# Loading w_mod in three pieces and c in two loads, at the head of a decode block

## The chip, the cores and the metric

The kernel runs on one core of a Trainium2 chip. The core has five engines that work side by side: TensorE (PE; its weight loads are listed as PEld), VectorE (DVE), ScalarE (ACT), GpSimd (POOL) and SyncE (SP). 16 DMA engines move data between the chip's main memory (HBM) and the core's on-chip memory (SBUF, 128 partitions). The metric is the device time of one execution in microseconds, as the median of several runs.

## The reference

One block of a transformer in decode: 2 batch rows of 512 numbers each, adaptive layer norm from a condition `c`, attention over the last 4096 positions of a cache, and a feed-forward network.

```python
mod = (silu(c) @ w_mod).reshape(2, 6, 1, 512)        # w_mod: 512 x 3072
sa, ca, ga, sb, cb, gb = (mod[:, i] for i in range(6))
h = layernorm(x) * (1 + ca) + sa
q = h @ wq                                           # 512 x 4096: 32 heads of 128
o = softmax(q k^T / sqrt(128)) v                     # 8 K/V heads, last 4096 of 32768 positions
x = x + ga * (o @ wo)                                # 4096 x 512
h = layernorm(x) * (1 + cb) + sb
out = x + gb * (silu(h @ w1) @ w2)                   # 512 x 1792, 1792 x 512
```

All numbers are 32-bit floats. The weights and the part of the cache that is read come to about 97.5 MB, and each byte is used for two batch rows only.

## The kernel before

All large operands pass through one ring in SBUF: the tile `slots`, eight slots of 4096 floats in each of the 128 partitions. `stream(n)` hands out the next n slots (a pair or a group of four starts at a multiple of its size). `load_runs` (the load is line 93) loads `per` consecutive rows of a weight matrix into each partition; `load_pair` (line 82) loads two heads of the K or V cache. All these loads are issued on SP's queue, in the order in which the program names them, and a load whose slots are still in use waits on SP until the last reader is done. So SP's order is: w_mod (three slots), x, wq (slots 4 to 7), then K and V pairs by turns, wo in two parts, w1 in two, w2 in four, and the output.

For `w_mod`, partition p takes rows 4p to 4p+3, that is 4 x 3072 floats or 49,152 bytes which lie together in HBM. The view `wm[:, k, :]` is the k-th of these four rows.

`c` and `x` are small and are laid out with 128 columns in a few partitions of the tile `xc`, which a memset on DVE (line 100) clears first. Row b of `c` goes to partitions 16b, 16b+32, 16b+64 and 16b+96. Before the change, each batch row is loaded by two DMAs of two partitions (lines 105 and 106), issued on ACT's queue; x follows on SP's queue (line 109), behind w_mod.

The head of the computation is a chain. DVE transposes c into `cT` (line 261, in the helper `turned`), `silu_exp` (lines 228 to 231) and line 267 make `scT = silu(c)` transposed. Then PE multiplies it with w_mod: for each k, four products into `m_a` (line 275: the two modulations that the first norm needs, columns 0 to 1023 of the row) and four into `m_sp` (line 278: the other four, columns 1024 to 3071). After k = 0 the moments of x are put in between. DVE makes `h_a` (lines 286 to 290) and its transpose `hq_T`, and PE multiplies it with wq (line 308). Then the attention runs over eight steps, each with one K pair and one V pair: DVE transposes K (line 367), PE makes the scores (line 380), and after the softmax PE weights V (line 454). At the end come the products with wo (line 584), w1 (line 623) and w2 (line 657 for its first eight parts, lines 667 and 682 for the rest), the last element-wise work on DVE (lines 690 to 698) and the store (line 700).

The order on each engine around the change is the program's, as the scheduler of the tile framework lays it out. It waits for each reader's data by region of a tile. The first slots of the ring are reused by the first K pair, so SP's third large load waits for the products at lines 275 and 278.

Of the kernel before, what the change touches and what calls it, by code (L numbers as in the profile page):

```python
# [13 lines left out]
P = 128  # L14
B, D = 2, 512
# [8 lines left out]
def adaln_block(  # L24
# [19 lines left out]
    nc = tc.nc  # L44
# [16 lines left out]
    def const(shape, name):  # L61
        return consts.tile(shape, F32, name=name)

    def bank(tag, name):
        return (psum1 if tag in "CO" else psum).tile([P, 512], F32, tag=tag, name=name)
# [4 lines left out]
    def stream(n=1):  # L70
        i = turn_of[0]
        if n % 2 == 0:
            i += -i % n
        turn_of[0] = i + n
        return slots[:, i % RING : i % RING + n, :].rearrange("p s e -> p (s e)")
# [12 lines left out]
    def load_runs(w, per, lo, hi):  # L88

        e = w.shape[1]  # L90
        n = -(-(hi - lo) * e // 4096)
        t = stream(n)[:, : (hi - lo) * e].rearrange("p (q e) -> p q e", e=e)
        nc.sync.dma_start(t, w.rearrange("(p q) e -> p q e", q=per)[:, lo:hi, :])
        return t


    x2 = x.rearrange("b s d -> (b s) d")
    xc = const([P, 2, P], "xc")
    x_sp, c_sp = xc[:, 0, :], xc[:, 1, :]
    nc.vector.memset(xc, 0.0)  # L100
    wm = load_runs(w_mod, 4, 0, 4)
    rows8 = lambda t: t.rearrange("(ab r) m -> ab r m", r=16)[:, 0, :]
    for b in range(B):
        for lo in (0, 2):
            nc.scalar.dma_start(
                c_sp.rearrange("(g y) m -> g y m", g=4)[lo : lo + 2, 16 * b, :],
                c[b].rearrange("(g m) -> g m", m=P)[lo : lo + 2],
            )
    nc.sync.dma_start(rows8(x_sp), x2.rearrange("b (g m) -> g b m", m=P))  # L109
    wqt = load_runs(wq, 4, 0, 4)  # L110

# [470 lines left out]
    for q in range(32):  # L582
        g = q % 4
# [71 lines left out]
    for tt in range(WIDE):  # L655
        g = tt % 4
# [7 lines left out]
    y = bank("D", "acc_y")[:, :P]  # L664
# [13 lines left out]
    for tt in range(11, T2):  # L678
        for h in range(2):
            for g in range(4):  # L680
                lo = g * P + h * H
# [46 lines left out]
```

## Time and profile before

| what | value |
|---|---|
| time, median of 3 runs | 235.58 us (235.47 to 235.92) |
| the profiled execution, first to last instruction (span) | 233.6 us |
| median less span | 2.0 us |
| PE busy | 163.9 us (70%) |
| DVE busy | 115.2 us (49%) |
| ACT busy | 33.5 us (14%) |
| SP's DMA queue, share of 16 engines' time | 97.2% |
| HBM read | 97.53 MB, 418 GB/s over the span |
| mean granted clock of TensorE | 0.925 |

The profile gives the profiled execution's time as its span; what lies around the span isn't in it. The span is cut into 40 slices of 5.84 us in the page's second part. A busy PE is not PE at its peak, since matmuls are pipelined. The time of a DMA runs from its issue, on the queue of the engine that issued it, to its landing, when the last of its bytes is in place; a load that is issued while earlier ones are still under way waits its turn behind them.

### The profile page before, as it was taken

Reading aid. Unit: us, or ns where it says so; the run is one execution under the profiler, and the core shown is the slowest. Engines: PE = TensorE matmul, PEld = TensorE weight load, DVE = VectorE, ACT = ScalarE, POOL = GpSimd, SP = SyncE. Lnnn points to the kernel's source line nnn. Section 1 sums busy time; section 2 is a strip of 40 time slices with the busy share of each in tenths; the row PEclk is TensorE's granted clock in tenths of the full one; section 3 lists DMA queues with packets and bytes.
Section 4 is the critical chain, followed back from the end, with each engine's and each line's share of the span. In section 5 each row is a group of like instructions: output and inputs, shape, how many; then the busy total and the mean of one; then the engine's idle time right before and its main releaser. Section 6 shows DMA issues by size and latency. Waiting matters only on the chain.

```text
span 233.6 us, 2452 instructions
## 1 busy us (share of the span) xinstructions
PE 163.9 (70%) x998; PEld 41.1 (18%) x998; DVE 115.2 (49%) x180; ACT 33.5 (14%) x90; POOL 10.1 (4%) x34
## 2 busy tenths in 40 slices
PE   0004906959697839797598769748759786799984
PEld 0001401301111111211110201201111122233322
DVE  0007230187894758695197189259559540200332
ACT  2000210000311120130310201111030041000321
POOL 3004610000000000000000000000000000000000
PEclk9999995999859985999979979999997999899999
DMA  7998998999999999999999999999999999989991
GB/s 269 438 551 359 404 494 359 446 445 415 410 432 449 446 443 404 421 438 446 449 438 404 426 431 449 449 421 410 424 449 449 443 424 438 466 356 438 423 409 63
DMA packets 3794, 97.68 MB, mean 418 GB/s; under 512 B 432, under 2 KB 456, under 8 KB 968
## 3 DMA queue, kind: packets, MB, share of 16 engines
q1 hardware_dynamic: 3768, 97.53, 97.2%
q8 instruction: 8, 0.13, 0.2%
q14 instruction: 2, 0.02, 0.0%
q10 hardware_dynamic: 16, 0.00, 0.0%
HBM read 97.53 MB, written 0.00 MB: 418 GB/s over the span
## 4 chain that ended last, share of the span: by engine, by line
DMA 61%; issue 17%; DVE 13%; PE 6%; POOL 0%; SPq 0%; POOLq 0%; ACT 0%; DVEq 0%
DMA slots<-in_A_k_cache_dram 22%; DMA slots<-in_A_wq_dram 15%; DMA slots<-in_B_w_dram 12%; DMA slots<-in_A_v_cache_dram 12%; DVE kT L367 11%; PE q L308 3%; PE o L454 2%; DVE zp L426 1%; PE acc_yw L657 1%; DVE xp L424 1%; PE acc_l L682 0%; PE acc_y L667 0%; DVE qT L321 0%; POOL qg L325 0%; SPq L109 0%
## 5 line engine op out<-in xcount | busy, mean ns | idle before, releaser
L367 DVE STREAM_TRANSPOSE kT<-slots 128x1024 f32<-128x1024 f32 x64 | 73.7, 1211 | 22.7 <-DMA slots<-in_A_k_cache_dram 22.6
L380 PE MATMUL s<-kT,qbd 128*32 128x512 f32 x256 | 68.5, 714 | 17.6 <-DVE kT L367 16.6
L454 PE MATMUL o<-slots,ptb 128*32 128x512 f32 x256 | 29.1, 595 | 1.1 <-DMA slots<-in_A_v_cache_dram 1.1
L380 PEld LDWEIGHTS s<-kT,qbd 128*32 128x32 f32 x256 | 9.8, 115 | 69.1 <-DVE kT L367 65.1
L275 PE MATMUL m_a<-slots,scT 128*32 128x256 f32 x32 | 4.4, 500 | 20.6 <-DVE scT L267 20.6
L308 PE MATMUL q<-slots,hq_T 128*32 128x512 f32 x64 | 9.3, 745 | 7.7 <-DMA slots<-in_A_wq_dram 7.7
L554 PE MATMUL junk<-quad,id 128*32 128x512 f32 x24 | 12.9, 672 | 0.0
L466 ACT ACTIVATE ob<-o,own 128x128 f32<-128x128 f32 x32 | 9.1, 368 | 23.9 <-PE o L454 23.9
L410 ACT COPY bias<-bp 128x1 f32<-128x1 f32 x8 | 1.3, 159 | 75.3 <-PE bp L408 75.3
L454 PEld LDWEIGHTS o<-slots,ptb 128*32 128x32 f32 x256 | 7.7, 109 | 16.3 <-issue 16.2
L390 DVE TENSOR_REDUCE mx<-s 128x1 f32<-128x512 f32 x8 | 5.5, 692 | 9.6 <-PE s L380 9.6
L441 ACT ACTIVATE ptb<-pT,odd 128x256 f32<-128x256 f32 x16 | 6.7, 477 | 23.1 <-PE pT L433 23.1
L474 PE MATMUL o_all<-ob,selh 128*64 128x512 f32 x16 | 8.7, 622 | 2.0 <-ACT ob L466 2.0
L426 DVE TENSOR_TENSOR zp<-xp,quarter 128x1024 f32<-128x1024 f32 x8 | 9.8, 1226 | 0.2
L261 DVE STREAM_TRANSPOSE cT<-xc 128x128 f32<-128x128 f32 x1 | 0.4, 402 | 16.8 <-DMA xc<-in_c_dram 16.8
L321 DVE STREAM_TRANSPOSE qT<-q 128x512 f32<-128x512 f32 x2 | 1.4, 716 | 13.8 <-PE q L308 11.9
L433 PE MATMUL pT<-zp,mix 128*32 128x256 f32 x64 | 5.9, 446 | 2.8 <-DVE zp L426 2.3
L584 PE MATMUL acc_o<-slots,oTn 128*32 128x512 f32 x64 | 7.7, 593 | 0.0
L600 DVE STREAM_TRANSPOSE aoT<-ao 128x128 f32<-128x128 f32 x1 | 0.3, 316 | 14.8 <-PE ao L571 14.8
L392 PE MATMUL mT<-ident,mx 128*1 128x128 f32 x16 | 3.0, 271 | 6.4 <-DVE mx L390 6.4
L424 DVE STREAM_TRANSPOSE xp<-pr 128x512 f32<-128x512 f32 x8 | 5.5, 685 | 3.4 <-ACT pr L412 3.4
L278 PE MATMUL m_sp<-slots,scT 128*32 128x512 f32 x32 | 6.6, 712 | 0.0
(138 smaller groups left out, 90.1 us busy)
## 6 DMA issues: line engine op xcount, KB each, us to landing
slots<-in_A_k_cache_dram SPq DMA_DIRECT2D x8, 4096.0 KB, 27.6
slots<-in_A_v_cache_dram SPq DMA_DIRECT2D x8, 4096.0 KB, 27.8
slots<-in_w_mod_dram SPq DMA_DIRECT2D x1, 6144.0 KB, 17.0
slots<-in_A_wo_dram SPq DMA_DIRECT2D x1, 6144.0 KB
slots<-in_B_w_dram SPq DMA_DIRECT2D x1, 2688.0 KB
slots<-in_A_wo_dram SPq DMA_DIRECT2D x1, 2048.0 KB, 29.5
slots<-in_B_w_dram SPq DMA_DIRECT2D x1, 2048.0 KB
slots<-in_B_w_dram SPq DMA_DIRECT2D x1, 896.0 KB
```

The lines of the kernel that those rows point to most:

```text
L278: nc.tensor.matmul(m_sp[r, :], scT[:, k, :], cd[:, g], start=(k == 0), stop=(k == 3))
L308: nc.tensor.matmul(q_ps[n][32 * g : 32 * g + 32, :], hq_T[:, k, :], wv[:, n, g], start=(k == 0), stop=(k == 3),)
L367: inorder(nc.vector.transpose(kT[s, j][:, 32 * c : 32 * c + 32, :], kt[s].rearrange("p (n j r) -> p j n r", j=4, r=32)[:, j, 32 * c : 32 * ...
L380: inorder(nc.tensor.matmul(s_ps[s][r : r + 32, :], qbd[h // 4][:, h % 4, b, j, :], kT[s, j][:, 32 * c : 32 * c + 32, e:32:2], start=(j == ...
L424: inorder(nc.vector.transpose(xp, pr[s]))
L426: inorder(nc.vector.tensor_mul(zp, xp[:, None, :, 0:16].to_broadcast([P, 4, 16, 16]), quarter[:, :, None, None].to_broadcast([P, 4, 16, 16 ...
L441: inorder(nc.scalar.activation(ptb[s % 2][:, :, e, :], tp.rearrange("p (w z) -> p w z", z=16), AF.Copy, scale=odd[:, e : e + 1],))
L454: inorder(nc.tensor.matmul(o_ps[s][r : r + 32, :], ptb[s % 2][:, w].rearrange("p e z -> p (e z)"), vt[s].rearrange("p (c w m f d) -> p c f ...
L466: inorder(nc.scalar.activation(o_sb[s][:, c], o_ps[s][:, c], AF.Copy, scale=own[:, m : m + 1]))
L474: inorder(nc.tensor.matmul(o_all, selh[:, lo : lo + 2 * HQ], o_sb[s], start=(s == 0), stop=(s == STEPS - 1)))
L554: inorder(nc.tensor.matmul(junk[0:32, :], id4, quad.rearrange("p m y -> p (m y)"), start=True, stop=True,))
L584: inorder(nc.tensor.matmul(acc[32 * g : 32 * g + 32, :], oTn[:, q, :], wot[q], start=(q < 4), stop=(q >= 28),))
```

## The change

A new function `load_mod` takes the place of `load_runs` for w_mod. It takes the same three slots, and fills them by three loads instead of one. Two of them bring the first 6,144 bytes (1536 floats, half of the first of the four rows) of each partition's part, one for the 64 even partitions and one for the 64 odd ones. The third brings the other 43,008 bytes of all 128 partitions. All three are issued on SP's queue, ahead of x and wq as before. Each batch row of c is loaded by one DMA of four partitions instead of two DMAs of two, on ACT's queue as before. The computation is the same.

```diff
+    def load_mod():
+        FIRST = 3 * D
+        t = stream(3)[:, : 4 * 6 * D]
+        runs = w_mod.rearrange("(p q) e -> p (q e)", q=4)
+        for parity in range(2):
+            nc.sync.dma_start(
+                t.rearrange("(u y) e -> u y e", y=2)[:, parity, :FIRST],
+                runs.rearrange("(u y) e -> u y e", y=2)[:, parity, :FIRST],
+            )
+        nc.sync.dma_start(t[:, FIRST:], runs[:, FIRST:])
+        return t.rearrange("p (q e) -> p q e", q=4)
...
-    wm = load_runs(w_mod, 4, 0, 4)
+    wm = load_mod()
     rows8 = lambda t: t.rearrange("(ab r) m -> ab r m", r=16)[:, 0, :]
     for b in range(B):
-        for lo in (0, 2):
-            nc.scalar.dma_start(
-                c_sp.rearrange("(g y) m -> g y m", g=4)[lo : lo + 2, 16 * b, :],
-                c[b].rearrange("(g m) -> g m", m=P)[lo : lo + 2],
-            )
+        nc.scalar.dma_start(
+            c_sp.rearrange("(g y) m -> g y m", g=4)[:, 16 * b, :],
+            c[b].rearrange("(g m) -> g m", m=P),
+        )
     nc.sync.dma_start(rows8(x_sp), x2.rearrange("b (g m) -> g b m", m=P))
     wqt = load_runs(wq, 4, 0, 4)
```

## The prediction

> **What bounds the kernel now.** I read the page first: the stretches, the queues, the chain that ended last. The first row below is the DMA rate in 40 slices of 5.84 us, the next the loads' queue, then instruction fetches, and the last two the chain by engine and by line.
>
> ```profile
> DMA  7998998999999999999999999999999999989991
> GB/s 269 438 551 359 404 494 359 446 445 415 410 432 449 446 443 404 421 438 446 449 438 404 426 431 449 449 421 410 424 449 449 443 424 438 466 356 438 423 409 63
> ...
> q1 hardware_dynamic: 3768, 97.53, 97.2%
> q8 instruction: 8, 0.13, 0.2%
> ...
> DMA 61%; issue 17%; DVE 13%; PE 6%; POOL 0%; SPq 0%; POOLq 0%; ACT 0%; DVEq 0%
> ```
>
> The 16 DMA engines are busy 97.2% of the span with SP's loads. Only the first slice (269 GB/s) and the last (63) are low. So the kernel is one stream of 97.53 MB, and its end is the start of the stream, plus bytes over rate, plus a tail. To see both ends I asked for busy time in chosen windows (last columns: granted clock, DMA share, GB/s).
>
> ```profile
> 0.00:1.70 1.70, 0.00 (x0) 0.00 (x0) 0.27 (x1) 0.00 (x0) 1.09 (x8) 1.00 0.00 0
> 1.70:2.00 0.30, 0.00 (x0) 0.00 (x0) 0.00 (x0) 0.00 (x0) 0.30 (x2) 1.00 5.38 1638
> 2.00:3.00 1.00, 0.00 (x0) 0.00 (x0) 0.00 (x0) 0.00 (x0) 0.50 (x1) 1.00 0.81 295
> 3.00:4.00 1.00, 0.00 (x0) 0.00 (x0) 0.00 (x0) 0.18 (x1) 0.00 (x0) 1.00 0.00 0
> 4.00:5.00 1.00, 0.00 (x0) 0.00 (x0) 0.00 (x0) 1.00 (x1) 0.00 (x0) 1.00 1.83 786
> 36.20:200.00 163.80, 126.71 (x694) 27.27 (x694) 101.04 (x119) 25.41 (x77) 0.97 (x4) 0.91 1.01 433
> 216.00:226.00 10.00, 9.07 (x56) 2.79 (x54) 3.74 (x18) 3.61 (x6) 0.00 (x0) 1.00 0.98 415
> 228.00:229.60 1.60, 1.60 (x53) 1.21 (x53) 0.09 (x1) 0.65 (x2) 0.00 (x0) 1.00 0.43 169
> ```
>
> A share above 1 shows that the view books a transfer whole in the window where it starts. That makes the start readable. One row of w_mod is 49,152 bytes. 1638 GB/s in 0.30 us is 491 KB, so 10 rows start by 2.0 us; 295 KB is 6 more by 3.0 us; 786 KB is the second row of all 16 engines, after 4.0 us. Durations follow: 5.38 x 16 x 0.30 / 10 = 2.58 us for each of the first ten, 0.81 x 16 / 6 = 2.16 us for the six late ones, 1.83 x 16 / 16 = 1.83 us in steady state. The cold start costs (10 x 0.75 + 6 x 0.33) / 16 = 0.59 us on an engine's mean, beside 1.7 us in which nothing flows. From 36.2 to 200 us the rate is 433 GB/s, and the sixteen loads of K and V (listed below) lie in that window, so loads queued behind each other leave no gap. 97.53 MB at 433 GB/s is 225.2 us; from 1.7 us that ends at 226.9, and in the window from 228 us engines still finish (share 0.43). An engine carries what it lost at the start to the end, since nothing lets it catch up.
>
> The chain in order of time gives the tail, and its beginning gives the head:
>
> ```profile
> 1.94 35.14 DMA slots<-in_A_wq_dram
> 37.08 0.14 issue
> 37.22 5.87 PE q L308 x32
> ...
> 197.16 29.02 DMA slots<-in_B_w_dram
> 226.17 0.14 issue
> 226.31 1.92 PE acc_yw L657 x16
> ...
> 230.79 0.14 DVEq L724
> ```
>
> The last matmuls start when the first part of w2 lands at 226.17. Of the waits below, PE waited 0.7 us for that load: compute there is that much ahead, and a stream that shifts by less shifts the end one to one.
>
> ```profile
> PE acc_yw L657 <- DMA slots<-in_B_w_dram: 0.7, 1, 0.7
> ```
>
> **The change part by part.** The head of the kernel, from the timeline (start, length, engine, line):
>
> ```profile
> 0.73 0.37 SPq L93 DMA_DIRECT2D slots<-in_w_mod_dram  x1
> 1.16 2.63 ACTq L105 DMA_DIRECT2D xc<-in_c_dram  x4
> 1.17 0.72 SPq L109 DMA_DIRECT2D xc<-in_A_x_dram  x1
> 1.94 0.58 SPq L93 DMA_DIRECT2D slots<-in_A_wq_dram  x1
> 17.91 0.40 DVE L261 STREAM_TRANSPOSE cT<-xc 128x128 f32<-128x128 f32 x1 [16.78 <-DMA xc<-in_c_dram]
> 20.55 1.08 PE L275 MATMUL m_a<-slots,scT 128*32 128x256 f32 x8 [20.55 <-DVE scT L267]
> 28.30 1.83 SPq L82 DMA_DIRECT2D slots<-in_A_k_cache_dram  x2
> 29.91 0.40 DVE L261 STREAM_TRANSPOSE hq_T<-h_a 128x128 f32<-128x128 f32 x1
> ```
>
> The page's list of issues has the time from issue to landing in its last column:
>
> ```profile
> slots<-in_A_k_cache_dram SPq DMA_DIRECT2D x8, 4096.0 KB, 27.6
> slots<-in_A_v_cache_dram SPq DMA_DIRECT2D x8, 4096.0 KB, 27.8
> slots<-in_w_mod_dram SPq DMA_DIRECT2D x1, 6144.0 KB, 17.0
> ```
>
> *c earlier.* c is issued from 1.16 us and arrives at 17.9, with the whole of w_mod (0.73 + 17.0 = 17.7). Half as many loads, beside rows of 6,144 bytes instead of 49,152, should pass much sooner; I take 4 to 10 us. DVE then finishes scT (now 17.91 to 20.5, so 2.6 us of work) before w_mod has landed, and m_a starts at 17.7 instead of 20.55: 2.8 us sooner. The four first matmuls of k = 0 read only columns 0 to 1023 and could start on the first two loads, but the next ones read columns up to 3071 and wait for the third. What follows moves by those 2.8 us: the K loads' issue from 28.30 to 25.5, hq_T from 30.3 to 27.5. Neither is late now. The projection at line 308 waits for wq until 37.08, 6.8 us after hq_T; the K loads stand behind wq in the queue. Worth 0.0 us; cover gone would mean that hq_T came later than 37.08.
>
> The Trainium skill's page "DMA: Bandwidth & Descriptors" (section "Queues, rings and completion order") says that a DMA engine takes turns between queues packet by packet. That would explain c's arrival with w_mod and its gain here; the sum is zero with or without it.
>
> *Two more issues on SP.* They stand ahead of x's and wq's issue. At 0.37 to 0.72 us each these move by 0.7 to 1.4 us; wq goes out by 3.4 us and is first needed when w_mod's bytes are through, after 17 us. Cost 0. ACT issues two c loads fewer, 2.63 / 4 = 0.66 us each, and is done issuing at 2.5 instead of 3.8 us; its first work needs cT and comes later in both.
>
> *More and shorter rows.* 128 x 6,144 bytes = 786 KB, 1.82 us of stream. In 216 to 226 us, where rows are mostly shorter (16 KB and less, by the shapes of w1 and w2), the rate per busy share is 415 / 0.98 = 423, against 433 / 1.01 = 429: 1.4% worse, +0.03 us on that piece. With the completions of two further loads I take +0.03; bounds 0 and 0.1.
>
> *The start of the stream.* This is the term that counts, and no row of before shows a first load of 64 rows. The first byte comes 1.7 - 0.73 = 1.0 us after the issue; I keep that, since SP's order ahead of it is unchanged. Then come the 0.59 us. Lower bound: all of it stems from the first load's size, and short first rows remove it: -0.6, and the six engines that start up to 1 us late come level, worth another 0.3 at most: -0.9. Upper bound: none goes, and the next loads come too late for the engines (below): +0.9. I take the part nearest to a row: half as many rows let the six late engines start with the others, and 6/16 x 0.33 = -0.12 us; the cold cost of the other ten, which started within 0.3 us of each other, stays.
>
> The sum: 0.0 + 0.0 + 0.03 - 0.12 = -0.09 us on the span of 233.6. The span stands 2.0 us below the median of the runs, 235.58; I leave that difference as it is. 235.58 - 0.09 = 235.49, say 235.5.
>
> **The rivals.**
>
> *A shorter start (faster).* The cold 0.59 us hang on the 49 KB rows or on the 128 rows of the first load. For it: the six latest starters took 2.16 us, the early ones 2.58, so it isn't a constant price per engine. Against: a latency of the first read would be there for any size. Price -0.6 + 0.03: 235.0; with level engines 234.7.
>
> *A hole behind the short loads (slower).* Place: the DMA engines between 2 and 5 us. The third load is the third issue on SP, where wq is now, at 1.94 us; plus 1.0 us to the first byte and up to 1.3 us until the last engine has some (1.7 to 3.0 now) is 2.9 to 4.2 us. The two short ones keep an engine busy from 1.7 for 1.82 + 0.59 us, until 4.1. So it fits by 0 to 1.2 us, and from a first byte later than 4.1 us on the engines run dry, each 0.1 us at full price. For it: x's issue took 0.72 us beside ACT's c loads against 0.37 for the one before them, so issues hold each other up, and if the second and third each slip by the 0.72 of an issue, the late engines' 4.2 becomes 5.6 against the 4.8 at which they (from 3.0, without the early ones' excess) would be done: +0.8. I price it at +0.6, between 0.4 and 0.9: 236.2.
>
> *Halves that collide (slower).* If with every other partition two DMA engines write through one port, the 1.82 us of the short loads double: +1.8, 237.4. No row shows a load of every other partition. Against: engines drift apart by themselves.
>
> The Trainium skill's page "SBUF — State Buffer" (section "Door 1: The DMA port swizzle (why `[64,N]` ≈ `[32,N]`)") assigns groups of four partitions to ports; even or odd partitions touch all 16, as contiguous halves would not. By that rule the collision needn't come, though it depends on which engine gets which rows.
>
> *Each load starts anew (slower).* If an engine's next load begins only when the one before it is complete, the two further loads pay the 1.0 us from issue to first byte again: +2.0, 237.6. Against it stands the 433 GB/s of the K and V loads, which follow each other without such gaps.
>
> That case has a rule of the Trainium skill for it, in "DMA: Bandwidth & Descriptors", section "Rules for kernel authors": two transfers to disjoint halves of the partitions gain nothing and should be one over 128. The page's fixed cost is about 2 us a transfer, so by its figure, an estimate, the price would be 4 us.
>
> *The 2.8 us arrive at the end (faster).* If c's wait were on the path, 232.8. Against it stand the 6.8 us of slack at line 308 and the full queue.
>
> *c comes no sooner.* Then the head stays at 20.55 and the time as in the forecast.
>
> **How the numbers follow.** What this kernel's measurement can tell from no change is about 0.2%, 0.47 us. Forecast, start moves by less than that (235.1 to 236.0): 0.50, with the case that c comes no sooner in it. Shorter start: 0.26. Hole: 0.16. Collision: 0.04. Each load anew: 0.02. The 2.8 us at the end: 0.02. Faster than 235.11: 0.26 + 0.02 and a little of the forecast's edge, 0.29. Slower than 236.05: 0.16 + 0.04 + 0.02, 0.22. Within: 0.49. The range takes in the shorter start with level engines and the hole with its bound, 234.7 to 236.5; outside are the collision, the loads that start anew, the 2.8 us and little else.
>
> **What would show it.** Right: 10 to 16 engines start by 2.0 us with short rows, the window 2 to 5 us shows a steady share, c's transpose runs before 12 us, m_a starts near 17.7 by the landing of w_mod, and line 308 still waits for wq, at about 37. Shorter start: wq lands before 36.7, and w2's first part before 225.7. Hole: a window between 2.5 and 5 us with a low DMA share, and wq later than 37.4. Collision: the short rows take twice 1.83 / 8 = 0.23 us. Wrong altogether: PE's wait at line 657 goes from a load to another engine, so that the tail is compute's.

## The result: slower by 1.0%

Beside each other the two kernels took 235.55 us before (median; 235.27 to 236.42) and 237.75 us after (237.36 to 238.69). The ratio is 1.0096, with a 95% interval of 1.0081 to 1.0112, so the change costs 2.2 us. The forecast was 235.5 us, within a range of 234.7 to 236.5. The profiled execution of after took 237.83 us, with a span of 236.1 against 233.6. Executions of one kernel fall on two levels some 0.8 us apart (of the kernel first128 below, six of ten at 235.41 to 235.49 us and four at 236.18 to 236.38), so small differences of medians are read together with the time at which wq lands. The new lines shift the others by 12: line 308 is now 320, line 657 is now 669.

First the page of after, with the DMA rate in 40 slices (of 5.90 us now) and SP's queue:

```profile
GB/s 228 408 401 518 389 500 344 430 433 429 433 439 439 430 422 433 439 425 433 439 439 427 427 432 439 427 427 433 436 427 439 433 461 408 439 405 424 428 363 24
...
q1 hardware_dynamic: 3928, 97.53, 96.4%
```

The queue moved the same 97.53 MB. Its transfers took 0.964 x 236.1 = 227.6 us on an engine's mean, against 0.972 x 233.6 = 227.1 before. Idle were 8.5 us against 6.5. So four fifths of the longer span is time in which DMA engines stood still, and a fifth is transfers that took longer. The first slice has 228 GB/s instead of 269, and the last two have 363 and 24 instead of 409 and 63. The engines lost unequally and finish further apart: in windows of half a microsecond the stream thins out from 229.0 to about 232.0 us, where before it took from 228.0 to 229.5.

The windows of after show the place (the last columns are the granted clock, the DMA share and GB/s; a transfer is booked whole where it starts):

```profile
1.70:2.00 0.30, 0.00 (x0) 0.00 (x0) 0.00 (x0) 0.00 (x0) 0.30 (x2) 1.00 0.00 0
2.00:3.00 1.00, 0.00 (x0) 0.00 (x0) 0.00 (x0) 0.17 (x1) 0.50 (x1) 1.00 0.70 160
3.00:4.00 1.00, 0.00 (x0) 0.00 (x0) 0.00 (x0) 1.00 (x1) 0.00 (x0) 1.00 1.08 401
4.00:5.00 1.00, 0.00 (x0) 0.00 (x0) 0.00 (x0) 0.11 (x1) 0.00 (x0) 1.00 1.65 639
5.00:6.00 1.00, 0.00 (x0) 0.00 (x0) 0.00 (x0) 0.00 (x0) 0.00 (x0) 1.00 0.41 147
6.00:7.00 1.00, 0.00 (x0) 0.00 (x0) 0.00 (x0) 0.00 (x0) 0.00 (x0) 1.00 1.58 518
...
36.20:200.00 163.80, 126.10 (x692) 27.20 (x692) 100.56 (x118) 24.44 (x74) 0.97 (x4) 0.91 1.00 433
```

Three things are to be seen. Nothing has started by 2.0 us, where ten rows had before. All 128 short rows are 786 KB, and for what has come of c and x (4 KB each) I add 6 KB; by 6.0 us 160 + 401 + 639 + 147 = 1347 KB have started, so (1347 - 792) / 43.0 = 13 long rows. In windows of 0.01 us the first of them starts at 4.47 us and the last short row at 5.33; a long row takes 1.6 us or more, so none of the 13 is an engine's second. Three of the 16 engines still have none, though the short rows are out. And the 12 rows that start between 6 and 7 us (518 / 43.0) take 1.58 x 16 / 12 = 2.11 us each, where a row of 43,008 bytes takes 1.83 x 43.0 / 49.2 = 1.60 at the rate of before. In the middle of the kernel the rate is 433 GB/s as it was.

The chain of after, in order of time, shows the loss carried to the end:

```profile
3.44 36.13 DMA slots<-in_A_wq_dram
39.57 0.14 issue
...
199.77 28.88 DMA slots<-in_B_w_dram
228.65 0.14 issue
...
233.34 0.14 DVEq L736
```

wq lands at 39.57 instead of 37.08, 2.49 us later; the first part of w2 at 228.65 instead of 226.17, 2.48 later; the last piece starts at 233.34 instead of 230.79, 2.55 later. Everything is lost before wq lands. Of the waits of after, these two are the ones that the forecast leaned on:

```profile
PE q L320 <- DMA slots<-in_A_wq_dram: 10.2, 1, 10.2
...
PE acc_yw L669 <- DMA slots<-in_B_w_dram: 0.6, 1, 0.6
```

The head of after, from its timeline:

```profile
0.73 1.20 SPq L103 DMA_DIRECT2D slots<-in_w_mod_dram  x2
1.16 1.64 ACTq L117 DMA_DIRECT2D xc<-in_c_dram  x2
1.98 0.68 SPq L107 DMA_DIRECT2D slots<-in_w_mod_dram  x1
...
10.60 0.40 DVE L273 STREAM_TRANSPOSE cT<-xc 128x128 f32<-128x128 f32 x1 [9.47 <-DMA xc<-in_c_dram]
13.23 1.08 PE L287 MATMUL m_a<-slots,scT 128*32 128x256 f32 x8 [13.23 <-DVE scT L279]
20.25 1.93 PE L290 MATMUL m_sp<-slots,scT 128*32 128x512 f32 x8 [5.94 <-DMA slots<-in_w_mod_dram]
28.24 1.84 SPq L82 DMA_DIRECT2D slots<-in_A_k_cache_dram  x2
29.85 0.40 DVE L273 STREAM_TRANSPOSE hq_T<-h_a 128x128 f32<-128x128 f32 x1
```

c comes 7.3 us sooner and the first products start at 13.23 instead of 20.55. But the next ones wait for the third load, which lands at 20.2, 2.5 us later than w_mod did; so hq_T is where it was, and waits for wq as before.

### The profile page after: what moved, and what is told of

It is laid out like the page before. It is cut to its first block, busy times and chain, and to the rows that moved or that the text cites. A ratio compares the mean times of both kernels' runs of the same rounds, so it can differ in the third digit from the quotient of the medians.

```text
span 236.1 us, 2453 instructions
## 1 busy us (share of the span) xinstructions
PE 165.7 (70%) x998; PEld 41.8 (18%) x998; DVE 115.3 (49%) x180; ACT 33.5 (14%) x90; POOL 10.1 (4%) x34
## 3 DMA queue, kind: packets, MB, share of 16 engines
q1 hardware_dynamic: 3928, 97.53, 96.4%
HBM read 97.53 MB, written 0.00 MB: 413 GB/s over the span
## 4 chain that ended last, share of the span: by engine, by line
DMA 61%; issue 17%; DVE 13%; PE 6%; SPq 1%; POOL 0%; POOLq 0%; ACT 0%; DVEq 0%
DMA slots<-in_A_k_cache_dram 22%; DMA slots<-in_A_wq_dram 15%; DMA slots<-in_B_w_dram 12%; DMA slots<-in_A_v_cache_dram 12%; DVE kT L379 11%; PE q L320 2%; PE o L466 2%; DVE zp L438 1%; PE acc_yw L669 1%; DVE xp L436 1%; SPq L103 0%; PE acc_l L694 0%; PE acc_y L679 0%; DVE qT L333 0%; POOL qg L337 0%
## 5 line engine op out<-in xcount | busy, mean ns | idle before, releaser
L392 PE MATMUL s<-kT,qbd 128*32 128x512 f32 x256 | 67.3, 683 | 17.3 <-DVE kT L379 16.2
L466 PE MATMUL o<-slots,ptb 128*32 128x512 f32 x256 | 30.8, 625 | 1.2 <-DMA slots<-in_A_v_cache_dram 1.2
L287 PE MATMUL m_a<-slots,scT 128*32 128x256 f32 x32 | 5.7, 524 | 13.2 <-DVE scT L279 13.2
L290 PE MATMUL m_sp<-slots,scT 128*32 128x512 f32 x32 | 7.2, 825 | 5.9 <-DMA slots<-in_w_mod_dram 5.9
L466 PEld LDWEIGHTS o<-slots,ptb 128*32 128x32 f32 x256 | 8.1, 114 | 17.7 <-issue 17.6
L420 PE MATMUL bp<-negscale,mrow 1*128 1x1 f32 x16 | 3.0, 254 | 4.3 <-DVE mrow L413 4.3
```

Of the source, the lines that this page charges most:

```text
L290: nc.tensor.matmul(m_sp[r, :], scT[:, k, :], cd[:, g], start=(k == 0), stop=(k == 3))
L392: inorder(nc.tensor.matmul(s_ps[s][r : r + 32, :], qbd[h // 4][:, h % 4, b, j, :], kT[s, j][:, 32 * c : 32 * c + 32, e:32:2], start=(j == ...
L466: inorder(nc.tensor.matmul(o_ps[s][r : r + 32, :], ptb[s % 2][:, w].rearrange("p e z -> p (e z)"), vt[s].rearrange("p (c w m f d) -> p c f ...
```

## The experiments

All diffs are against the changed kernel, and all kernels compute the whole reference. Each was timed beside the kernel before, whose median was 235.48 to 235.68 us. Three theories stood at the start: the hole (the long load's rows reach the engines after the short ones are done), the collision (half loads, or short rows, are slow in themselves; a later form of it is called stalled rows), and the crowd (the mere number of early issues holds up the start).

**Which part of the change.** c's two loads alone, c_only:

```diff
-    wm = load_mod()
+    wm = load_runs(w_mod, 4, 0, 4)
```

> c in two loads of four partitions, w_mod in one load as before. Three theories of the 2.2 us lost. Hole: the engines run dry because the third load of w_mod comes too late behind two short ones. Collision: rows of a load over every other partition are written slower, so the loss grows with the bytes loaded that way. Crowd: the mere number of issues on SP and ACT in the first 3 us holds up the start. Hole and collision expect no change from before here, 235.3 to 235.8 us; crowd expects a gain, since two issues fewer remain: 235.0 to 235.4. c itself should arrive sooner than 17.9 us, at about 12, since each DMA engine has four packets of c instead of eight.

w_mod's three loads alone, mod_only:

```diff
-        nc.scalar.dma_start(
-            c_sp.rearrange("(g y) m -> g y m", g=4)[:, 16 * b, :],
...
+        for lo in (0, 2):
+            nc.scalar.dma_start(
+                c_sp.rearrange("(g y) m -> g y m", g=4)[lo : lo + 2, 16 * b, :],
...
```

> w_mod in three loads, c in four loads as before. Hole and collision expect the whole loss, 237.5 to 238.0 us. Crowd expects more than that, 238.2 to 238.8, since ACT issues two loads more beside SP's.

c_only took 235.67 us, ratio 1.0011 [0.9998, 1.0024]; mod_only 238.33, 1.0117 [1.0096, 1.0139]. The timeline of c_only, then the chain of mod_only:

```profile
12.38 0.40 DVE L273 STREAM_TRANSPOSE cT<-xc 128x128 f32<-128x128 f32 x1 [11.24 <-DMA xc<-in_c_dram]
...
27.84 0.40 DVE L273 STREAM_TRANSPOSE hq_T<-h_a 128x128 f32<-128x128 f32 x1
```

```profile
4.42 34.97 DMA slots<-in_A_wq_dram
```

Half as many c loads bring c 5.5 us and hq_T 2.1 us sooner, and the time doesn't move, where the crowd expected a gain. The loss is in w_mod's part: there wq lands at 39.39, no later than in the changed kernel. Its median, 238.33 us, is above what the hole expected and in the crowd's range. But in its profiled execution PE starts the products with w2 at 229.58, 0.8 us later than in the changed kernel, and no longer waits for the load: what this execution loses beyond the changed kernel's is lost in PE's work before the end, not at the head.

**The halves.** One load of 128 rows for the first 6,144 bytes in place of two of 64, first128:

```diff
-        for parity in range(2):
-            nc.sync.dma_start(
-                t.rearrange("(u y) e -> u y e", y=2)[:, parity, :FIRST],
...
+        nc.sync.dma_start(t[:, :FIRST], runs[:, :FIRST])
```

> The first 6,144 bytes of all 128 partitions by one load, the rest by a second, c in two loads. Hole expects a part of the loss, since the rest is the second issue instead of the third and comes 0.6 us sooner: 235.8 to 236.6 us. Collision expects all of the loss to go: 235.4 to 235.8. Crowd expects half: 236.3 to 236.9.

235.48 us, 1.0008 [0.9995, 1.0021]: no loss, with the same short rows. That speaks against the crowd, which short_last below refutes: it has all the issues of the change and no loss. The hole's range is missed, too, since I had expected a part of the loss to stay; taken alone, this run speaks for the collision, and the runs with longer halves below decide. Its windows, and from its timeline the issue of the long load:

```profile
1.70:2.00 0.30, 0.00 (x0) 0.00 (x0) 0.00 (x0) 0.00 (x0) 0.30 (x2) 1.00 1.83 225
2.00:3.00 1.00, 0.00 (x0) 0.00 (x0) 0.00 (x0) 0.17 (x1) 0.51 (x1) 1.00 0.66 215
3.00:4.00 1.00, 0.00 (x0) 0.00 (x0) 0.00 (x0) 1.00 (x1) 0.00 (x0) 1.00 0.94 393
4.00:5.00 1.00, 0.00 (x0) 0.00 (x0) 0.00 (x0) 0.11 (x1) 0.00 (x0) 1.00 1.90 799
```

```profile
1.18 0.41 SPq L103 DMA_DIRECT2D slots<-in_w_mod_dram  x1
```

By 5.0 us 0.3 x 225 + 215 + 393 + 799 = 1475 KB have started, (1475 - 792) / 43.0 = 16 long rows: each engine has one. The same sum for after, 1200 KB, gives 9.5; counted in windows of 0.01 us they are 10, with three short rows still to come. The long load is issued at 1.18 here and at 1.98 there. These rows also answer the shorter start: the first 11 short rows (67.5 / 6.14) take 1.83 x 0.3 x 16 / 11 = 0.80 us against 0.23 in steady state (0.94 x 16 / 64), an excess of 0.57 us. The first ten long rows of before had an excess of 2.58 - 1.83 = 0.75. So most of the excess isn't a matter of the row's size, and no start was to be gained.

**More cover.** The halves kept, with 12,288 bytes of each partition's part (first_12k) and with 24,576 (long_first, `12 * D`):

```diff
-        FIRST = 3 * D
+        FIRST = 6 * D
```

> As the changed kernel, with 12,288 bytes of each partition in the two loads over even and odd partitions. Hole (some engines get their first rows of the third load too late): the two loads last 1.8 us longer, so about all of the loss but the later start goes: 235.8 to 236.6 us. Rival, stalled rows (short rows of the loads over every other partition are held up on some engines, whatever follows them): as many rows as in the changed kernel, so the same loss: 237.4 to 238.0.

> As the changed kernel, but the two loads over even and odd partitions bring 24,576 bytes of each partition instead of 6,144, and the third the other 24,576. Hole expects the third load to be in time, since the two before it last 7 us: only the later start is left, 235.8 to 236.3 us. Collision expects the loss to grow with the bytes: 241 to 246. Crowd expects the same loss as the changed kernel, 237.4 to 238.0.

first_12k: 235.78 us, 1.0010 [0.9994, 1.0025]. long_first: 236.64, 1.0039 [1.0026, 1.0051], above what the hole expects and far below the collision's 241; its wq lands at 37.64 like first_12k's at 37.63, so what it loses beyond first_12k isn't lost at the head, and stays open. With the short rows lasting longer than the third load takes to arrive, most of the loss is gone. What stays of first_12k's wq (0.55 us behind 37.08) includes the later start: here too nothing starts before 2.0 us.

**Shorter rows.** 2,048 bytes, in halves (first_2k) and, with the edit of first128 beside this one, as one load (first128_2k):

```diff
-        FIRST = 3 * D
+        FIRST = D
```

> The same with 2,048 bytes. Hole: the cover shrinks by 1.2 us, so the loss grows by about as much: 238.4 to 239.3 us. Stalled rows: as many rows as in the changed kernel, 237.2 to 238.0.

> As first128 (one short load over all partitions, then the rest), with 2,048 bytes instead of 6,144. The short load lasts only 0.6 us. Hole by the time of issue alone: the rest is issued at 1.18 us and reaches all engines by 2.2 to 3.5, while the short load ends at 2.9: 235.4 to 236.0 us. If what matters is that few rows stand ahead of the long ones, no loss: 235.3 to 235.7.

first_2k: 236.48 us, 1.0046 [1.0028, 1.0063]; first128_2k: 235.60, 0.9995 [0.9981, 1.0009]. first_2k was a miss: with cover for only a third as long the loss is half, not more. If the third load arrived at a fixed time after its issue, the engines would have run dry for longer.

**Position against form.** Three full-width loads (3,072 bytes, 3,072 and the rest) in place of the halves, three_full:

```diff
-        for parity in range(2):
...
+        nc.sync.dma_start(t[:, : FIRST // 2], runs[:, : FIRST // 2])
+        nc.sync.dma_start(t[:, FIRST // 2 : FIRST], runs[:, FIRST // 2 : FIRST])
```

> Three loads of w_mod again, but each over all 128 partitions: 3,072 bytes, 3,072 bytes and the rest. The cover ahead of the third load is that of the changed kernel. If the number of issues ahead of the third load makes the hole, a good part of the loss stays: 236.2 to 237.4 us. If it is the form of the half loads (their issues take 0.57 us instead of 0.39, and the first byte comes 0.36 us later), it goes: 235.4 to 235.8.

The three loads of the change with the long one first, short_last:

```diff
+        nc.sync.dma_start(t[:, FIRST:], runs[:, FIRST:])
         for parity in range(2):
...
-        nc.sync.dma_start(t[:, FIRST:], runs[:, FIRST:])
```

> The same three loads of w_mod as in the changed kernel, with the order turned: the long one (43,008 bytes of all partitions) first, then the two short ones. Hole: behind 12.7 us of long rows every later load is in time, so the loss goes: 235.4 to 235.9 us. Stalled rows, or anything that lies in the form of the short loads: the loss stays, 237.0 to 238.0.

c on SP's queue behind x instead of on ACT's, c_late:

```diff
+    nc.sync.dma_start(rows8(x_sp), x2.rearrange("b (g m) -> g b m", m=P))
     for b in range(B):
-        nc.scalar.dma_start(
+        nc.sync.dma_start(
...
-    nc.sync.dma_start(rows8(x_sp), x2.rearrange("b (g m) -> g b m", m=P))
```

> As the changed kernel, but c's two loads stand on SP's queue between x and wq, so that ACT issues nothing beside SP's first three issues. If the issues of ACT and SP hold each other up, the third load comes sooner and the loss shrinks: 236.0 to 237.0 us. If they don't, 237.4 to 238.0. c arrives with x, at about 18 us, and m_a starts at about 21, which alone costs nothing.

three_full: 237.49 us, 1.0073 [1.0049, 1.0098], with the long load issued at 1.63. short_last: 235.65, 1.0003 [0.9988, 1.0018]. c_late: 237.89, 1.0098 [1.0062, 1.0133]. Full-width loads lose too, and half loads behind the long one lose nothing: it is where the long load stands, not the form of the short ones. ACT's issues of c have no part in it. In c_late wq's issue, right behind the long load, came 1.0 us later too, at 4.47, without a gain.

**Another queue.** The long load on ACT's queue ahead of c, rest_on_act:

```diff
-        nc.sync.dma_start(t[:, FIRST:], runs[:, FIRST:])
+        nc.scalar.dma_start(t[:, FIRST:], runs[:, FIRST:])
```

> As the changed kernel, with the long third load issued on ACT's queue ahead of c instead of on SP's behind the two short ones. Hole: it is issued at about 0.75 us instead of 1.98, and an engine has its rows from a second queue when the short ones run out: 235.4 to 236.1 us. Stalled rows: 237.2 to 238.0. c then waits in ACT's queue behind the long load, as late as before (17 to 18 us), which costs nothing.

The odd half on ACT's queue, so that the long load is SP's second, odd_on_act:

```diff
-            nc.sync.dma_start(
+            (nc.sync, nc.scalar)[parity].dma_start(
```

> As the changed kernel, but the load over the odd partitions is issued on ACT's queue, beside the even one on SP, and the long load is the second on SP, at about 1.36 us instead of 1.98. If the time of issue decides, the hole closes: 235.6 to 236.5 us. If two large loads ahead of the third decide, wherever they are issued, the loss stays: 237.2 to 238.2.

odd_on_act: 235.69 us, 1.0009 [0.9997, 1.0021]. Its windows and the issue:

```profile
2.00:3.00 1.00, 0.00 (x0) 0.00 (x0) 0.00 (x0) 0.00 (x0) 1.00 (x4) 1.00 0.96 209
3.00:4.00 1.00, 0.00 (x0) 0.00 (x0) 0.00 (x0) 0.85 (x1) 0.27 (x1) 1.00 0.93 350
4.00:5.00 1.00, 0.00 (x0) 0.00 (x0) 0.00 (x0) 0.44 (x1) 0.00 (x0) 1.00 2.06 873
```

```profile
1.37 0.56 SPq L107 DMA_DIRECT2D slots<-in_w_mod_dram  x1
```

(1432 - 792) / 43.0 = 15 long rows by 5.0 us: with the half loads kept and the long one issued 0.6 us sooner, the hole is all but closed. wq lands at 37.43, and I put the 0.35 us that are left down to the start, which is that of after (nothing before 2.0 us).

rest_on_act took 237.24 us, 1.0063 [1.0046, 1.0079], where I had expected no cost. The head has no hole, but c stood behind the long load on ACT's queue. From its timeline, then its windows:

```profile
23.87 0.40 DVE L273 STREAM_TRANSPOSE cT<-xc 128x128 f32<-128x128 f32 x1
...
34.35 1.84 SPq L82 DMA_DIRECT2D slots<-in_A_k_cache_dram  x2
35.97 0.40 DVE L273 STREAM_TRANSPOSE hq_T<-h_a 128x128 f32<-128x128 f32 x1
```

```profile
36.00:37.00 1.00, 0.00 (x0) 0.00 (x0) 1.00 (x4) 0.23 (x1) 0.53 (x1) 1.00 1.12 393
37.00:38.00 1.00, 0.61 (x8) 0.34 (x12) 0.29 (x1) 0.00 (x0) 0.20 (x1) 1.00 0.80 295
```

c's cover was used up: the first K loads, which wait for the slots of w_mod, were issued at 34.35 instead of 28.30, and between 36 and 38 us 344 GB/s on the mean start instead of 433. Long rows that are issued late behind a full stream and leave engines dry: this looks like the head's hole at another place, but no run tests that.

**Issue time, count and traffic.** The rows of first128 with x's issue in between, so that the long load is the third issue again: x_between, and with FIRST = D (2,048 bytes) x_between_2k.

```diff
-        for parity in range(2):
...
+        nc.sync.dma_start(t[:, :FIRST], runs[:, :FIRST])
+        nc.sync.dma_start(rows8(x_sp), x2.rearrange("b (g m) -> g b m", m=P))
         nc.sync.dma_start(t[:, FIRST:], runs[:, FIRST:])
...
-    nc.sync.dma_start(rows8(x_sp), x2.rearrange("b (g m) -> g b m", m=P))
```

> As first128 (one short load of 6,144 bytes over all partitions, then the rest), with x's small load issued between the two, so that the rest is the third issue on SP, at about 1.9 us. If being issued third and later decides, a hole as in the changed kernel: 236.3 to 237.7 us. If large loads ahead decide, none: 235.3 to 235.8.

> As x_between (a short load over all partitions, x, then the rest at about 1.9 us), with 2,048 bytes in the short load instead of 6,144, so that the engines move little between 2.3 us and the arrival of the rest. If the rest's arrival is a matter of its time of issue alone, it still comes at 5.5 to 6.3 us on half the engines, whose cover now ends 1.2 us sooner: 238.5 to 239.5 us. If the traffic ahead slows it, it comes by 4.0 on all, 1 us after the short load ends: 235.9 to 236.9.

Three full-width loads of 2,048 bytes ahead of the rest, four_full:

```diff
-        for parity in range(2):
...
+        for i in range(3):
+            r = slice(i * D, (i + 1) * D)
+            nc.sync.dma_start(t[:, r], runs[:, r])
```

> Three short loads of 2,048 bytes over all partitions, then the rest: the bytes ahead of the long load are those of three_full, in one load more. If each large load ahead delays the long one, the loss is larger than three_full's 2.0 us: 237.8 to 239.0. If only the time of issue decides, it is issued 0.45 us later than in three_full: 237.7 to 238.2. If the bytes ahead decide, the same as three_full: 237.0 to 237.7.

x_between: 237.84 us, 1.0098 [1.0076, 1.0119], as slow as the change from one issue moved. Its wq lands 1.97 us later than before, against 2.49 in the change; as in mod_only, PE then no longer waits for w2 in the profiled execution, so some 0.5 us of its loss is PE's at the end. four_full: 237.35, 1.0083 [1.0068, 1.0099], no more than three_full though its long load is the fourth. x_between_2k: 236.40, 1.0041 [1.0022, 1.0059]. The windows of x_between and the issue, then the same of x_between_2k:

```profile
1.70:2.00 0.30, 0.00 (x0) 0.00 (x0) 0.00 (x0) 0.00 (x0) 0.30 (x2) 1.00 1.53 225
2.00:3.00 1.00, 0.00 (x0) 0.00 (x0) 0.00 (x0) 0.17 (x1) 0.50 (x1) 1.00 0.72 209
3.00:4.00 1.00, 0.00 (x0) 0.00 (x0) 0.00 (x0) 1.00 (x1) 0.00 (x0) 1.00 1.01 412
4.00:5.00 1.00, 0.00 (x0) 0.00 (x0) 0.00 (x0) 0.11 (x1) 0.00 (x0) 1.00 1.20 449
5.00:6.00 1.00, 0.00 (x0) 0.00 (x0) 0.00 (x0) 0.00 (x0) 0.00 (x0) 1.00 0.76 258
```

```profile
1.94 0.59 SPq L104 DMA_DIRECT2D slots<-in_w_mod_dram  x1
```

```profile
1.70:2.00 0.30, 0.00 (x0) 0.00 (x0) 0.00 (x0) 0.00 (x0) 0.30 (x2) 1.00 0.72 130
2.00:3.00 1.00, 0.00 (x0) 0.00 (x0) 0.00 (x0) 0.17 (x1) 0.51 (x1) 1.00 0.69 223
3.00:4.00 1.00, 0.00 (x0) 0.00 (x0) 0.29 (x1) 1.00 (x1) 0.00 (x0) 1.00 2.42 760
```

```profile
1.97 0.55 SPq L104 DMA_DIRECT2D slots<-in_w_mod_dram  x1
```

In x_between (1138 - 792) / 43.0 = 8 long rows have started by 5.0 us, and 14 by 6.0 ((1396 - 792) / 43.0): at two engines they start over 4.0 us after the issue. In x_between_2k, with the issue at the same time but 262 KB of short rows instead of 786, (1022 - 268) / 47.1 = 16 have started by 4.0: none later than 2.0 us after the issue. The order, the number and the time of the issues are the same, and the traffic ahead differs.

**The halves laid out otherwise.** The lower and the upper 64 partitions instead of the even and the odd, with FIRST = 6 * D (12,288 bytes), low_high_12k:

```diff
-        FIRST = 3 * D
+        FIRST = 6 * D
...
-        for parity in range(2):
...
+        for half in range(2):
+            r = slice(64 * half, 64 * half + 64)
+            nc.sync.dma_start(t[r, :FIRST], runs[r, :FIRST])
```

> As first_12k (two loads of 64 rows of 12,288 bytes, then the rest), but over partitions 0 to 63 and 64 to 127 instead of even and odd. If the partitions that a load covers don't matter, the rows take 460 ns as there and the time is 235.6 to 236.1 us. If a load over one contiguous half is written at half the rate, a row takes about 920 ns, the two loads 3.7 us more, and the time is 238.8 to 239.8.

239.51 us, 1.0146 [1.0111, 1.0181]. One window of low_high_12k, and the same of first_12k:

```profile
4.00:5.00 1.00, 0.00 (x0) 0.00 (x0) 0.00 (x0) 0.11 (x1) 0.00 (x0) 1.00 0.97 197
```

```profile
4.00:5.00 1.00, 0.00 (x0) 0.00 (x0) 0.00 (x0) 0.11 (x1) 0.00 (x0) 1.00 1.05 444
```

Rows of 12,288 bytes take 0.97 x 16 / 16 = 0.97 us in contiguous halves (197 KB is 16 rows) and 1.05 x 16 / 36 = 0.47 us in even and odd ones (444 KB is 36). The Trainium skill's page "SBUF — State Buffer" (section "Door 1: The DMA port swizzle (why `[64,N]` ≈ `[32,N]`)") has 64 contiguous partitions reach half of the ports; by that rule the halves' rate should halve, and the trace agrees. The even and odd halves of the change don't pay this.

**wq out of the way.** wq's load moved from SP, to stand behind the first products on ACT's, wq_late:

```diff
-    wqt = load_runs(wq, 4, 0, 4)
...
+    nc.scalar.dma_start(wqt, wq.rearrange("(p q) e -> p q e", q=4))
```

> As the changed kernel, but wq's load is issued on ACT's queue behind the exponential of c, at about 11 us instead of 3.4. If the issue of wq's load right behind the third load slows the third one's arrival, the loss shrinks to the later start: 235.7 to 236.3 us. If not, 237.4 to 238.2.

251.49 us, 1.068 [1.0661, 1.0699], and no answer: by its timeline the scheduler put the load first on ACT's queue, where it shared the engines with w_mod and held c back.

```profile
0.74 0.38 ACTq L280 DMA_DIRECT2D slots<-in_A_wq_dram  x1
```

Six kernels with 6,144 short bytes in each partition beside each other: the issue of the long load, its place among SP's issues, the first window with rows, the long rows that have started by 5.0 us (counted in windows of 0.01 us), wq's landing in the profiled execution, and the ratio of the runs. The profiled execution of three_full is its fastest.

| kernel | issue | place | first rows | long rows by 5.0 | wq lands | ratio |
|---|---|---|---|---|---|---|
| first128 | 1.18 | 2 | before 2.0 | 16 | 37.09 | 1.0008 |
| odd_on_act | 1.37 | 2 | after 2.0 | 15 | 37.43 | 1.0009 |
| three_full | 1.63 | 3 | before 2.0 | 13 | 38.81 | 1.0073 |
| x_between | 1.94 | 3 | before 2.0 | 8 | 39.05 | 1.0098 |
| changed kernel | 1.98 | 3 | after 2.0 | 10 | 39.57 | 1.0096 |
| four_full | 2.11 | 4 | before 2.0 | 7 | 39.03 | 1.0083 |

The later the long load is issued, the fewer engines have a row of it by 5.0 us, roughly. Its place among SP's issues goes along with the time. Among the three kernels where it is third, the earliest issue has the most rows, which speaks for the time; but they differ in what stands ahead of it too, so which of the two counts isn't shown.

## Why the prediction was wrong

**What bounds the kernel** was right. A stream that was 2.49 us late when wq landed ended 2.5 us late, with the old rate in between, and line 669 still waits 0.6 us for its load.

**c earlier** was right in its worth, 0 (c_only). Its size was a little off (10.6 us instead of 4 to 10), and the 2.8 us that I moved the K loads and hq_T by weren't there: I had left w_mod's landing at 17.7, and it went to 20.2.

**Two more issues on SP, cost 0**, is the step that failed. I priced the delay of x and wq, which are needed late, and left the long load's own delay, from 0.73 to 1.98 us, to a rival of 0.16. The cost of the change lies there, in place of the 0 some 2.1 us of the 2.49 by which wq is late: x_between differs from first128 only in that x is issued ahead of the long load, which moves from 1.18 to 1.94 and from second to third, and the ratio goes from 1.0008 to 1.0098.

**The start of the stream** was wrong in sign. I kept 1.0 us from the issue to the first byte, because SP's order ahead of it is the same. But the issue of a half load takes 0.6 us (1.20 for two) where the load of 128 rows took 0.37, and no row starts before 2.0 us. In odd_on_act, where little else is left, wq is 0.35 us late, and so in place of -0.12 the term is about +0.35, by one profiled execution of each kernel. The gain of the rival with the shorter start, the cold 0.59 us, isn't there either (first128: the excess is 0.57 with rows an eighth as long).

**The rivals.** The hole had the mechanism and roughly the place (it forecast 2.5 to 5 us and wq later than 37.4; in after the share is low at 5 to 6), with a price that was too small, 0.4 to 0.9 us. What was mis-sized is the arrival: I worked out 2.9 to 4.2 us from the start of an idle chip (1.0 us to the first byte, 1.3 for the spread), and allowed for 5.6. In x_between two engines, and in after three, had no long row at 6.0 us. And I hadn't thought of the rows after the hole, 2.11 us instead of 1.60. The loss of after, 2.49 us at wq, is thus, as an estimate, some 0.35 for the later start, and 2.1 for the hole with its slow rows; how these two share it on the engine that ends last, the views don't tell. The collision is refuted by first_12k's 0.47 us a row, and by odd_on_act. Against "each load starts anew" stand four_full, with one load more than three_full and no more loss, and first128, with one more than before and none. The Trainium skill's rule that I set beside that rival, in "DMA: Bandwidth & Descriptors", section "Rules for kernel authors", advises one transfer over 128 partitions in place of two to halves of them. first128, which does that, loses nothing; but odd_on_act and short_last keep the halves and lose nothing either. The estimate of 4 us, from the page's fixed cost of each transfer, isn't what the runs show: four_full's further load cost nothing.

**What stays open** is why the long load's rows come late when the engines are busy with rows of 6,144 bytes. The runs show that the long load's issue (its time or its place on SP, which no run parts cleanly) and the traffic ahead decide; what holds the rows back in between, none of them shows. The page "DMA: Bandwidth & Descriptors" of the Trainium skill (section "Latency and other measured facts") gives an access to HBM 0.2 us on average and 2 us at high load. That points the same way as x_between beside x_between_2k, but no run here tells such a latency from another cause. No kernel tried was faster than the one before by more than the measurement can tell; first128_2k, at 0.9995 [0.9981, 1.0009], comes nearest.

## What to carry to other kernels

In a kernel that is one DMA stream, a small load put ahead of a large one can cost more than it brings, through the delay of the large one (behind 6,144 short bytes, a delay of 0.45 or 0.64 us cost nothing here, one of 0.9 us or more 0.7 to 1.0%): count the time from there to its first row on the last engine, and let what is queued ahead last longer. Take that time from a place where the engines are busy, not from the start of the kernel. And before a load is split to bring something sooner, look whether that something is waited for: c came 7 us sooner here, and 6.8 us of slack stood behind it.

## What the runs showed of the hardware that I had not expected

- From a load's issue to its first row on the last engine passed at most 2.3 us on idle engines (before: issue at 0.73, all 16 by 3.0), at most 2.0 us behind 262 KB of short rows (x_between_2k), and over 4.0 us behind 786 KB of them, on two engines of x_between.
- A first load of 64 rows holds SP for 0.6 us instead of 0.37, and its first byte comes after 2.0 us instead of before.
- On the ten or eleven engines that start by 2.0 us, the first row takes longer than later ones by 0.57 us where it has 6,144 bytes (first128: 0.80 against 0.23) and by 0.75 where it has 49,152 (before: 2.58 against 1.83).
- A load into every other partition runs at full rate, one into 64 contiguous partitions at about half (0.47 and 0.97 us for a row of 12,288 bytes, where a quarter of a 49,152-byte row of before takes 1.83 / 4 = 0.46).
